# A fused attention and dense kernel: the probability product as one run of 56 matmuls, and priority shifts by step

## Chip, core and metric

The kernel runs on one core of a Trainium2 chip. The metric is the device time of one execution in microseconds (us); below, PE is TensorE, PEld its weight load, DVE VectorE, ACT ScalarE, POOL GpSimd and SP the SyncE queue that issues the DMAs.

## What is computed

```python
scores = scale * np.matmul(q, k.transpose(0, 1, 3, 2))     # 4 batches, 8 heads, 576 x 64
thresh = np.max(scores, axis=-1, keepdims=True) - tau
scores = np.where(scores >= thresh, scores, -1000000000.0)
attn = np.exp(scores - np.max(scores, axis=-1, keepdims=True))
attn = attn / (np.sum(attn, axis=-1, keepdims=True) + 1e-09)
x = np.matmul(attn, v)            # then heads side by side: 2304 tokens x 512
...
h = (x @ w1) * (x @ w2) @ w3      # 512 -> 1024 -> 1024
x = h @ w_out                     # 1024 -> 512
h = x @ w_in                      # 512 -> 2048
out = (h * (1.0 / (1.0 + np.exp(-h)))) @ w_out2
```

## The kernel before

**Stages.** The work is four batches of attention and then four groups of tokens through the dense layers. `merge` puts them in five stages: attention of batch 0 beside the product of w3 and w_out (line 1477); attention of batches 1, 2 and 3, each beside the dense layers of the group before; and the last group alone. In the profile the stages meet near 147, 378, 548 and 728 us.

**Attention.** Heads go in 16 pairs, four to a batch. A tile of 128 score rows is four or eight matmuls (line 867) into one of two PSUM buffers; DVE takes the maximum (line 834), ACT and DVE do mask and exponential (lines 900 to 926), then ACT and DVE write the probabilities as a high and a low half in 16 bits (lines 967 and 974), and SP's queue transposes them into the tiles `pt` (lines 985 and 994). When all tiles of a pair are there, `pv` (line 1009) multiplies them by the values: 14 chunks (9 of the high values, 5 of the low) x 2 halves of the tokens x 2 heads, 56 matmuls of 128 x 64 against 288 columns in 16 bits (line 1039). The two heads write the two halves of the partitions of one bank. ACT and DVE copy the result out as the next layer's input (lines 1063, 1078 and 1085).

**Dense layers.** They run in fp32r with each operand split in a high and a low part, three matmuls of 128 x 128 against 288 or 432 columns for each product (line 1426, and line 1376 in the last stage). Weights are split by ACT and POOL or DVE (lines 541, 565 and 559).

**Who sets the order.** Every operation is given to a planner with an engine, a duration and a priority. `Plan.run` simulates all engines: at each step it takes, of all operations whose inputs and buffers are there, the one that can start earliest, and among equal starts the one with the lowest priority number, which is the operation's place on a time scale of the stage (`plan.base`, in us of TensorE work). It leaves no engine idle while something is ready for it. The order so found is the fixed order of each engine's instructions on the chip. Only the order is taken over; the chip keeps its own time.

`pv` gives its 56 matmuls to the planner as five operations, of 3, 3, 3, 3 and 2 chunks, all with the same inputs and the same two banks. An operation that follows another one on PE is ready 3 ns after it:

```python
LATENCY = {
    ("PE", "PE"): 3, ("PE", "ACT"): 127, ("PE", "DVE"): 103,
```

The duration that the plan gives such an operation comes from

```python
def mm(n, width, f32r=False):
    return n * (width * 0.4517 + 2.9 if f32r else width * 0.4167 + 2.5) + 3
```

that is 1.03 x 738 = 760 ns for one of three chunks and 508 ns for the one of two, 3.55 us in all.

`merge` lays the steps of the attention and those of the dense layers over the same stretch of the time scale. Then it moves each step by a number of `SHIFTS`: eight numbers for the attention steps of a stage and eight for the dense ones, each for an eighth of the steps. A step is for example "the scores of two tiles", "the product of one pair" or "one output block of a dense layer"; the shift moves the priority of all its operations, on all engines and on SP's queue.

Of the kernel before, what the change touches and what calls it, by code (L numbers as in the profile page):

```python
# [17 lines left out]
HALF = S // 2  # L18
# [54 lines left out]
    (  # L73
        (3, -4, -5, -5, -15, -15, -6, 7),
        (-4, -3, 15, 9, 9, 0, -11, -4),
    ),
)

# [280 lines left out]
def fused_kernel(  # L359
# [11 lines left out]
    nc = tc.nc  # L371
    plan = Plan()
# [151 lines left out]
    def mm(n, width, f32r=False):  # L524
        return n * (width * 0.4517 + 2.9 if f32r else width * 0.4167 + 2.5) + 3
# [10 lines left out]
    def act_op(kind, n, fn, r, w, hold=(), ns=110):  # L536
        plan.op(kind, "ACT", ns + n * 0.833, fn, r, w, hold)
# [37 lines left out]
    def part_of(view):  # L575
        b = Buf()
        b.tile = view
        return b
# [5 lines left out]
    vst = [part_of(vs_all[:, j]) for j in range(2)]  # L584
    k_vx = [Buf(), Buf()]
# [423 lines left out]
    def pv(pr):  # L1009

        b, k = pr // NP, pr % NP
        got = [pts.pop(2 * pr + j) for j in range(2)]
        vs = vps[pr][1]
        ps = [m_b(1), m_b(1)]
        more = [p for p, _ in got]
        for g2, *_ in PLACES[b]:  # L1020
            if (g2, k) not in xs:
                new = x2_b if g2 == 2 else x_b
                xs[g2, k] = new(), new()
                more.extend(xs[g2, k])
        if b == 1:
            xs[2, k] = x2_b(), x2_b()
        if b == 2:
            wide[k] = x32_b()
        if b > 1:
            more.append(wide[k])  # L1030
        cs = [*((c, c) for c in range(9)), *((9 + c, c) for c in range(5))]
        for n0 in range(0, len(cs), 3):
            part = cs[n0:n0 + 3]

            def prods(part=part):
                for n, c in part:
                    for a in range(2):
                        for j in range(2):
                            nc.tensor.matmul(  # L1039
                                out=ps[a].t[64 * j:64 * j + 64, 0:HALF], lhsT=vst[j].t[:, n, :],  # L1040
                                rhs=got[j][0].t[:, c, a * HALF:(a + 1) * HALF],
                                start=(n == 0), stop=(n == len(cs) - 1),
                            )

            plan.op(
                "pv", "PE", 1.03 * mm(2 * len(part), HALF), prods,
                [*got[0][1], *got[1][1], *vst, *k_vx], ps, hold=more if n0 == 0 else more[:2],
            )

        def scales():  # L1050
            for i in range(2):
                m = slice(64 * i, 64 * i + 64)
                nc.vector.tensor_copy(out=vs.t[m, 8:9], in_=vs.t[m, 6 + i:7 + i])

        plan.op("v scale", "DVE", 140, scales, [vs], [vs])
        for a in range(2):
            if b == 3 or b == 2 and a == 1:
                at = HALF * (a + 1) if b == 3 else 0
                key = Buf()
                wkeys.setdefault(k, []).append(key)  # L1060
                act_op(
                    "x up", HALF,
                    lambda a=a, at=at: nc.scalar.activation(
                        out=wide[k].t[:, at:at + HALF], in_=ps[a].t[:, 0:HALF], func=ACTF.Copy,
                        scale=vs.t[:, 8:9],
                    ),
                    [ps[a], vs], [key], [wide[k]], ns=163,
                )
                continue
            (g2, c0, _, at), = PLACES[b]  # L1070
            at += a * HALF - c0
            xh, xl = xs[g2, k]
            kh, kl = Buf(), Buf()
            cut = slice(at, at + HALF)
            xkeys.setdefault((g2, k), []).append((at, at + HALF, kh, kl))
            act_op(
                "xh", HALF,
                lambda a=a, cut=cut, xh=xh: nc.scalar.activation(
                    out=xh.t[:, cut], in_=ps[a].t[:, 0:HALF], func=ACTF.Copy, scale=vs.t[:, 8:9],
                ),  # L1080
                [ps[a], vs], [kh], [xh], ns=163,
            )
            plan.op(
                "xl", "DVE", 436,
                lambda a=a, cut=cut, xh=xh, xl=xl: nc.vector.scalar_tensor_tensor(
                    out=xl.t[:, cut], in0=ps[a].t[:, 0:HALF], scalar=vs.t[:, 8:9],
                    in1=xh.t[:, cut].bitcast(F32), op0=ALU.mult, op1=ALU.subtract,
                ),
                [ps[a], kh, vs], [kl], [xh, xl],
            )  # L1090
        if b == 3 and k % 2:
            quads = [
                (
                    Buf(lambda _, w=w, i=i: wide[w].t[:, i * WIDE:(i + 1) * WIDE]),
                    wkeys[w][i:i + 2], wide[w],
                )
                for w in (k - 1, k) for i in range(2)
            ]
            xcs.append(combine(quads))
# [25 lines left out]
    def combine(quads):  # L1125

        (b11, n11, h1), (b12, n12, _), (b21, n21, h2_), (b22, n22, _) = quads
        hold = [*dict.fromkeys(x for x in (h1, h2_) if x is not None)]  # L1130
        psum = b11.tag == "m"

        def sub(out, a, b, need):
            plan.op(
                "c sub in PSUM" if psum else "c sub", "DVE", 75 + WIDE * 1.042,
                lambda: nc.vector.tensor_tensor(
                    out=tile_of(out), in0=tile_of(a), in1=tile_of(b), op=ALU.subtract
                ),
                [a, b, *need], [out], hold,
            )  # L1140

        if psum:
            s11, t1, t2 = u_b(), u_b(), u_b()
            plan.op(
                "y out", "ACT", 75 + WIDE * 0.833,
                lambda: nc.scalar.activation(out=s11.t, in_=tile_of(b11), func=ACTF.Copy),
                [b11], [s11],
            )
        else:
            s11, t1, t2 = b11, b12, b22  # L1150
        got = {"B11": parts(b11, n11, hold)}
        sub(t1, b12, s11, [*n12, *n11])
        got["B22"] = parts(b22, n22, hold)
        sub(t2, b22, t1, n22)
        got["T2"] = parts(t2, [], hold)
        sub(b11, t2, b11, n11)
        got["T3"] = parts(b11, [], hold)
        got["T1"] = parts(t1, [], hold)
        got["B21"] = parts(b21, n21, hold)
        sub(b21, b21, t2, n21)  # L1160
        got["T4"] = parts(b21, [], hold)
        return got

    def move_x(k):

        key = xkeys[1, k][1][2:]
        new = Buf(), Buf()
        c0, c1 = MOVED
        for a, b, k0, k1 in zip(xs[1, k], xs[2, k], key, new):
            act_op(  # L1170
                "x move", c1 - c0,
                lambda a=a, b=b: nc.scalar.activation(
                    out=b.t[:, 0:c1 - c0], in_=a.t[:, c0:c1].bitcast(F32), func=ACTF.Copy
                ),
                [k0], [k1], [a, b],
            )
        xkeys.setdefault((2, k), []).append((0, c1 - c0, *new))
# [622 lines left out]
    def merge(a, m, lead):  # L1800

        plan.stage += 1
        shifts = SHIFTS[plan.stage]
        ta, tm = sum(c for c, _ in a) or 1.0, sum(c for c, _ in m) or 1.0
        base = plan.base
        jobs = []
        for t, steps, off, late in ((ta, a, lead, shifts[0]), (tm, m, 0.0, shifts[1])):
            at = 0.0
            for n, (c, fn) in enumerate(steps):
                jobs.append((at / t * (ta + tm) - off, len(jobs), fn, late[8 * n // len(steps)]))  # L1810
                at += c
        for at, _, fn, late in sorted(jobs, key=lambda x: x[:2]):
            plan.base = base + at + late
            fn()
        plan.base = base + ta + tm
# [7 lines left out]
    for b in range(len(GROUPS)):  # L1823
# [9 lines left out]
        if pairs:  # L1833
# [5 lines left out]
            for grp in range(4):  # L1839
                for i in range(2):  # L1840
                    c = slice(grp % 2 * 512, grp % 2 * 512 + 512)
                    n = 16 + grp // 2 * 4 + 2 * i
# [11 lines left out]
    plan.base = 0.0  # L1854
    w34s = [(0.0, load_wo)] + [(6.9, lambda f=f: w34_step(f)) for f in range(8)]
    merge(attn_steps(0), w34s, LEAD)
    for i in range(len(GROUPS)):
        steps = [(0.0, lambda k=k: move_x(k)) for k in range(NP)] if i == 1 else []
        merge(attn_steps(i + 1) if i + 1 < B else [], steps + moe_steps(i), LEADS[i])
# [55 lines left out]
```

## Time and profile before

| | |
|---|---|
| Median of 3 runs | 979.19 us (979.11 to 982.52) |
| Profiled execution | 981.1 us |
| Its span, first to last instruction | 979.3 us |
| PE busy | 934.6 us |
| DVE busy | 693.0 us |
| ACT busy | 675.4 us |
| POOL busy | 447.9 us |
| TensorE's granted clock, mean over the span | 0.98 of full |

Busy time is the time in which an engine had an instruction running; matmuls are pipelined, so that time lost between them can lie inside PE's busy time. The profiled execution's own time holds the span and what lies around it.

### The profile page before, as it was taken

What the parts mean: (1) busy time and instruction counts of PE and PEld (TensorE: products, weight loads), DVE (VectorE), ACT (ScalarE), POOL (GpSimd) and SP (SyncE); (2) the same over time, 40 slices, a digit from 0 to 9 for tenths busy, and PEclk for the clock granted to TensorE, in tenths of its full rate; (3) what the DMA queues carried; (4) which work ended last, traced back from release to release, by engine and by line L of the source; (5) the groups of instructions that cost most, each with busy time, mean ns of one, the idle gap of its engine ahead of it and who ended that gap; (6) DMA issues with size and microseconds to landing.
All of it is one profiled execution on the core that took longest, in us unless ns stands there. A gap on an engine that the chain in (4) does not pass through costs nothing.

```text
span 979.3 us, 16087 instructions
## 1 busy us (share of the span) xinstructions
PE 934.6 (95%) x5632; PEld 830.2 (85%) x5632; DVE 693.0 (71%) x1488; ACT 675.4 (69%) x1217; POOL 447.9 (46%) x271
## 2 busy tenths in 40 slices
PE   4589999999999999999999999999999999999998
PEld 3455559989999989888889989899889999899998
DVE  6889676878887987666657766676459845856654
ACT  7989787878987877776878678887734423654331
POOL 1433233423341525575758567694776422423310
PEclk9589999999999999999999999999999999999999
DMA  8998999979899997787776878675632122111111
GB/s 247 244 257 231 254 298 306 268 215 279 256 257 259 241 251 217 174 208 182 171 173 181 235 170 207 176 182 139 140 123 85 44 67 85 44 65 65 51 36 73
DMA packets 216241, 175.13 MB, mean 179 GB/s; under 512 B 175584, under 2 KB 181728, under 8 KB 216160
## 3 DMA queue, kind: packets, MB, share of 16 engines
q1 hardware_dynamic: 216160, 174.10, 66.8%
q8 instruction: 44, 0.72, 0.3%
q14 instruction: 37, 0.30, 0.1%
HBM read 112.20 MB, written 19.40 MB: 134 GB/s over the span
## 4 chain that ended last, share of the span: by engine, by line
PE 75%; DVE 7%; DMA 6%; ACT 6%; issue 3%; POOL 1%; SPq 0%; ACTq 0%; DVEq 0%; POOLq 0%
PE banks L1426 45%; PE banks L1376 13%; PE banks L867 7%; PE banks L1039 7%; PE banks L1477 4%; DMA vr<-qkv 2%; DVE banks L834 2%; DMA pt<-hl 1%; DMA qk<-qkv 1%; DVE hm L974 1%; POOL lo L565 1%; DVE wr L1249 1%; DMA r<-w 1%; ACT banks L900 1%; ACT wr L1234 0%
## 5 line engine op out<-in xcount | busy, mean ns | idle before, releaser
L1426 PE MATMUL banks<-acts,hi 128*128 128x288 f32 (+1 forms) x1280 | 310.3, 330 | 0.8 <-ACT banks L900 0.8
L565 POOL TENSOR_TENSOR lo<-wr,hi 128x1024 fp32r<-128x1024 f32 x77 | 185.6, 2412 | 190.8 <-PE banks L1426 92.9
L1426 PEld LDWEIGHTS banks<-acts,hi 128*128 128x128 f32 x1280 | 219.0, 188 | 13.3 <-issue 7.0
L1426 PE MATMUL banks<-acts,lo 128*128 128x288 f32 (+1 forms) x640 | 209.3, 327 | 1.4 <-POOL lo L565 1.4
L867 PE MATMUL banks<-k,qs 128*128 128x288 f32 x640 | 122.8, 328 | 26.3 <-DVE e L926 8.8
L867 PEld LDWEIGHTS banks<-k,qs 128*128 128x128 f32 x640 | 100.0, 202 | 46.4 <-DVE e L926 8.7
L834 DVE TENSOR_REDUCE banks<-banks 128x1 f32<-128x576 f32 x144 | 107.0, 761 | 44.9 <-PE banks L867 43.3
L541 ACT ACTIVATE hi<-wr 128x1024 fp32r<-128x1024 f32 x96 | 101.9, 1062 | 33.9 <-DMA wr<-w 9.7
L1426 PEld LDWEIGHTS banks<-acts,lo 128*128 128x128 f32 x640 | 120.2, 188 | 5.3 <-POOL lo L565 2.4
L1426 PE MATMUL banks<-x,hi 128*128 128x288 f32 (+1 forms) x512 | 123.3, 329 | 0.0
L1426 PE MATMUL banks<-act3s,hi 128*128 128x432 f32 x384 | 106.8, 359 | 1.5 <-ACT act3s L1601 1.3
L565 POOL TENSOR_TENSOR acts<-tb,acts 128x432 fp32r<-128x432 f32 (+1 forms) x60 | 73.0, 1223 | 42.8 <-ACT acts L1515 35.2
L1426 PEld LDWEIGHTS banks<-x,hi 128*128 128x128 f32 x512 | 87.3, 188 | 3.8 <-issue 2.0
L565 POOL TENSOR_TENSOR qs<-qk,qs 64x576 fp32r<-64x576 f32 x31 | 45.4, 1463 | 95.7 <-ACT qs L661 77.0
L1426 PE MATMUL banks<-x,lo 128*128 128x288 f32 (+1 forms) x256 | 83.7, 327 | 1.4 <-POOL lo L565 1.1
L1426 PEld LDWEIGHTS banks<-act3s,hi 128*128 128x128 f32 x384 | 72.2, 188 | 5.4 <-ACT act3s L1601 1.6
L1039 PE MATMUL banks<-pt,vst 128*64 128x288 f16 x896 | 72.7, 297 | 4.3 <-DMA pt<-hl 3.6
L1039 PEld LDWEIGHTS <-vst 128*64 128x64 f16 x896 | 46.3, 112 | 30.0 <-issue 26.6
L1426 PE MATMUL banks<-act3s,lo 128*128 128x432 f32 x192 | 68.9, 359 | 0.0
L565 POOL TENSOR_TENSOR lo<-sums,hi 128x1024 fp32r<-128x1024 f32 x16 | 38.8, 2426 | 63.2 <-PE banks L1376 33.8
L1477 PE MATMUL banks<-wos,hi 128*128 128x512 f32 x128 | 62.8, 622 | 2.0 <-DVE hi L1249 2.0
L974 DVE SCALAR_TENSOR_TENSOR hl<-banks,st,hl 128x576 f16<-128x576 f32 x67 | 52.5, 811 | 16.2 <-ACT hl L967 16.0
(155 smaller groups left out, 1799.1 us busy)
## 6 DMA issues: line engine op xcount, KB each, us to landing
wr<-w SPq DMA_DIRECT2D x72, 512.0 KB, 3.8
qk<-qkv SPq DMA_DIRECT2D x31, 576.0 KB, 5.0
r<-wo SPq DMA_DIRECT2D x24, 512.0 KB, 6.2
w<-wr SPq DMA_DIRECT2D x24, 512.0 KB, 4.5
vr<-qkv SPq DMA_DIRECT2D x16, 576.0 KB, 5.3
r<-w3t SPq DMA_DIRECT2D x16, 512.0 KB, 6.1
r<-w SPq DMA_DIRECT2D x16, 512.0 KB, 7.5
r<-win SPq DMA_DIRECT2D x16, 512.0 KB, 6.8
```

What stands on the lines that cost most here:

```text
L541: kind, n, lambda: nc.scalar.activation(out=out(), in_=a(), func=ACTF.Copy), r, w, hold, ns
L565: lambda: nc.gpsimd.tensor_tensor(out=out(), in0=a(), in1=b(), op=ALU.subtract),
L834: lambda: nc.vector.tensor_reduce(out=low(), in_=sp.t[:, :, 0:HALF], axis=AX.XY, op=ALU.max, negate=True),
L867: nc.tensor.matmul(out=sp.t[:, a, 0:HALF], lhsT=q.t[:, o:o + 128], rhs=k.t[:, a * HALF:(a + 1) * HALF], start=(n == 0), stop=(n == len(mms ...
L900: lambda n=n, sp=sp, x=x: nc.scalar.activation(out=half2(x), in_=half2(sp), func=ACTF.Prelu, bias=col(1, n), scale=1.0, alpha=1.0e36,),
L974: lambda: nc.vector.scalar_tensor_tensor(out=two(hl.t[:, S:2 * S]), in0=src(), scalar=r(), in1=two(hl.t[:, 0:S]), op0=ALU.mult, op1=ALU.su ...
L1039: nc.tensor.matmul(out=ps[a].t[64 * j:64 * j + 64, 0:HALF], lhsT=vst[j].t[:, n, :], rhs=got[j][0].t[:, c, a * HALF:(a + 1) * HALF], start= ...
L1249: lambda: nc.vector.scalar_tensor_tensor(out=ri(), in0=low(), scalar=29, in1=ri(), op0=ALU.logical_shift_right, op1=ALU.bitwise_or,),
L1376: nc.tensor.matmul(out=ps.t[:, 0:n], lhsT=cut(w_), rhs=x_.t, start=(first and k == 0 and i == 0), stop=(k == len(quads) - 1 and i == 2), s ...
L1426: nc.tensor.matmul(out=ps.t[:, 0:n1 - n0], lhsT=a_.t[:, k * 128:(k + 1) * 128], rhs=x_.t[:, n0:n1], start=(n == 0 and i == 0), stop=(n == ...
L1477: lambda jb=jb, x=x: nc.tensor.matmul(out=ps.t[:, 0:512], lhsT=f32(r.t)[:, jb * 128:(jb + 1) * 128], rhs=x.t[:, 0:512].bitcast(F32), start ...
```

## The change

In `pv` the five operations become one, which issues all 56 matmuls one after the other. Its duration in the plan is the sum of its matmuls and 210 ns, 3.64 us. The operation holds all buffers that the five held between them.

In `merge` every step gets a further shift of its own, added to that of its eighth. These are the table `FINE`, some 310 numbers in the same unit, mostly between -30 and 30; its first and last lines are below. The operations, their engines and their number are else the same; the order of each engine's instructions is planned anew with both edits.

```diff
+FINE = (
+    (
+        (-22.5, 16, 2, 4, 5, 13, 5.5, 3.5, 1, 2, -1.5, -0.5, 1, 1.5, 1, 11.5,
...
+        (-10, 1, 5.5, 20.5, 10.5, 2.5, 0, 3.5, -12,),
+    ),
...
+    (
+        (),
+        (13, 8, 13, 28.5, 28.5, 22.5, 18.5, 19, 30, 34, 30.5, 37, 25.5, 11.5, -1, 32,
+         -57, 8, 24, -14.5, -18, -23, -66, -10, 5.5, 20, 58, 0, 8.5, 7,),
     ),
 )
...
         cs = [*((c, c) for c in range(9)), *((9 + c, c) for c in range(5))]
-        for n0 in range(0, len(cs), 3):
-            part = cs[n0:n0 + 3]
-
-            def prods(part=part):
-                for n, c in part:
-                    for a in range(2):
-                        for j in range(2):
-                            nc.tensor.matmul(
-                                out=ps[a].t[64 * j:64 * j + 64, 0:HALF], lhsT=vst[j].t[:, n, :],
-                                rhs=got[j][0].t[:, c, a * HALF:(a + 1) * HALF],
-                                start=(n == 0), stop=(n == len(cs) - 1),
-                            )
-
-            plan.op(
-                "pv", "PE", 1.03 * mm(2 * len(part), HALF), prods,
-                [*got[0][1], *got[1][1], *vst, *k_vx], ps, hold=more if n0 == 0 else more[:2],
-            )
+
+        def prods():
+            for n, c in cs:
+                for a in range(2):
+                    for j in range(2):
+                        nc.tensor.matmul(
+                            out=ps[a].t[64 * j:64 * j + 64, 0:HALF], lhsT=vst[j].t[:, n, :],
+                            rhs=got[j][0].t[:, c, a * HALF:(a + 1) * HALF],
+                            start=(n == 0), stop=(n == len(cs) - 1),
+                        )
+
+        plan.op(
+            "pv", "PE", mm(2 * len(cs), HALF) + 210, prods,
+            [*got[0][1], *got[1][1], *vst, *k_vx], ps, hold=more,
+        )
...
-        for t, steps, off, late in ((ta, a, lead, shifts[0]), (tm, m, 0.0, shifts[1])):
+        fine = FINE[plan.stage]
+        for t, steps, off, late, more in (
+            (ta, a, lead, shifts[0], fine[0]), (tm, m, 0.0, shifts[1], fine[1])
+        ):
             at = 0.0
             for n, (c, fn) in enumerate(steps):
-                jobs.append((at / t * (ta + tm) - off, len(jobs), fn, late[8 * n // len(steps)]))
+                jobs.append((
+                    at / t * (ta + tm) - off, len(jobs), fn, late[8 * n // len(steps)] + more[n]
+                ))
                 at += c
```

## Rows read from the trace of the kernel before

**Rows 1.** The page, part 1: busy us, share of the span and instructions of each engine.
```profile
PE 934.6 (95%) x5632; PEld 830.2 (85%) x5632; DVE 693.0 (71%) x1488; ACT 675.4 (69%) x1217; POOL 447.9 (46%) x271
```

**Rows 2.** The page, part 4: shares of the chain that ended last.
```profile
PE 75%; DVE 7%; DMA 6%; ACT 6%; issue 3%; POOL 1%; SPq 0%; ACTq 0%; DVEq 0%; POOLq 0%
```

**Rows 3.** Stretches by stage: busy us of each engine (instructions), granted clock, DMA.
```profile
core 0: us, PE busy (x) PEld busy (x) DVE busy (x) ACT busy (x) POOL busy (x), PEclk, DMA share, GB/s
0.00:75.00 75.00, 46.71 (x189) 31.99 (x190) 59.81 (x151) 64.90 (x119) 23.04 (x20) 0.77 0.93 250
75.00:147.40 72.40, 70.56 (x350) 38.19 (x348) 56.09 (x130) 62.58 (x116) 22.34 (x14) 0.98 0.99 262
147.40:378.00 230.60, 226.47 (x1758) 215.85 (x1757) 185.74 (x376) 186.36 (x346) 79.75 (x45) 1.00 0.95 258
378.00:548.00 170.00, 167.11 (x1024) 150.01 (x1024) 115.33 (x284) 129.83 (x226) 110.31 (x66) 1.00 0.75 185
548.00:728.00 180.00, 178.11 (x1071) 160.37 (x1070) 111.23 (x257) 133.00 (x235) 127.49 (x79) 1.00 0.68 170
728.00:979.30 251.30, 245.67 (x1249) 233.82 (x1247) 164.76 (x293) 98.77 (x180) 84.95 (x49) 1.00 0.19 63
```

**Rows 4.** TensorE's waits, whole span: line, releaser, us in total, times, longest.
```profile
PE banks L867 <- DVE e L926: 8.8, 5, 3.1
...
PE banks L867 <- DVE hm L974: 2.8, 3, 1.3
```

**Rows 5.** TensorE in order of time, one pair's probability product, third stage: start, us.
```profile
399.48 0.36 PE L1426 MATMUL banks<-x,lo 128*128 128x432 f32 x1
399.77 0.93 PE L1039 MATMUL banks<-pt,vst 128*64 128x288 f16 x12
400.62 0.66 PE L1426 MATMUL banks<-x,hi 128*128 128x432 f32 x2
...
403.91 0.78 PE L867 MATMUL banks<-k,qs 128*128 128x288 f32 x4
...
406.20 0.68 PE L1039 MATMUL banks<-pt,vst 128*64 128x288 f16 x8
406.81 0.66 PE L1426 MATMUL banks<-x,hi 128*128 128x432 f32 x2
```

**Rows 6.** The same view where two or three pieces stand together.
```profile
249.96 1.66 PE L1039 MATMUL banks<-pt,vst 128*64 128x288 f16 x24
251.55 0.53 PE L1426 MATMUL banks<-acts,hi 128*128 128x288 f32 x2
...
532.62 2.40 PE L1039 MATMUL banks<-pt,vst 128*64 128x288 f16 x36
534.94 0.79 PE L867 MATMUL banks<-k,qs 128*128 128x288 f32 x4
```

**Rows 7.** The same view, two matmuls of a product with no change of shape.
```profile
708.57 0.36 PE L1426 MATMUL banks<-acts,lo 128*128 128x432 f32 x1
708.77 0.56 PE L1426 MATMUL banks<-acts,hi 128*128 128x432 f32 x2
```

**Rows 8.** The same view, first and last of the 72 runs of line 1039.
```profile
39.97 0.45 PE L1039 MATMUL banks<-pt,vst 128*64 128x288 f16 x1
...
707.46 0.68 PE L1039 MATMUL banks<-pt,vst 128*64 128x288 f16 x8
```

**Rows 9.** TensorE in order of time, end of the first stage.
```profile
138.51 1.25 PE L1039 MATMUL banks<-pt,vst 128*64 128x288 f16 x12
141.56 0.90 PE L867 MATMUL banks<-k,qs 128*128 128x288 f32 x4 [1.80 <-DVE hl L974]
...
143.97 1.33 PE L867 MATMUL banks<-k,qs 128*128 128x288 f32 x4
145.23 2.27 PE L1039 MATMUL banks<-pt,vst 128*64 128x288 f16 x32
...
147.43 0.53 PE L1426 MATMUL banks<-x,hi 128*128 128x288 f32 x2
```

More of the change, by code (lines that the diff above doesn't have):

```diff
@@ L75 @@
         (-4, -3, 15, 9, 9, 0, -11, -4),
+    ),
+)
+FINE = (
+    (
[4 rows of a table added]
+    ),
+    (
[6 rows of a table added]
+    ),
+    (
[6 rows of a table added]
+    ),
+    (
[6 rows of a table added]
+    ),
+    (
+        (),
+        (13, 8, 13, 28.5, 28.5, 22.5, 18.5, 19, 30, 34, 30.5, 37, 25.5, 11.5, -1, 32,
+         -57, 8, 24, -14.5, -18, -23, -66, -10, 5.5, 20, 58, 0, 8.5, 7,),
     ),
@@ L1031, in pv @@
         cs = [*((c, c) for c in range(9)), *((9 + c, c) for c in range(5))]
-        for n0 in range(0, len(cs), 3):
-            part = cs[n0:n0 + 3]
-            def prods(part=part):
-                for n, c in part:
-                    for a in range(2):
-                        for j in range(2):
-                            nc.tensor.matmul(
-                                out=ps[a].t[64 * j:64 * j + 64, 0:HALF], lhsT=vst[j].t[:, n, :],
-                                rhs=got[j][0].t[:, c, a * HALF:(a + 1) * HALF],
-                                start=(n == 0), stop=(n == len(cs) - 1),
-                            )
-            plan.op(
-                "pv", "PE", 1.03 * mm(2 * len(part), HALF), prods,
-                [*got[0][1], *got[1][1], *vst, *k_vx], ps, hold=more if n0 == 0 else more[:2],
-            )
+        def prods():
[10 more added lines that the diff above has]
+            [*got[0][1], *got[1][1], *vst, *k_vx], ps, hold=more,
+        )
         def scales():
```

20 rows, old and new, of the table FINE are left out of this document.

## Prediction

> **What bounds the kernel now.** I read the page's busy shares first, then its chain, then the busy time by stage, then TensorE's waits, and last TensorE in order of time around line 1039. TensorE (PE) is busy 95% of the span and no other engine over 71% [rows 1]; three quarters of the chain that ended last is PE's own work [rows 2]. By stage [rows 3] the picture splits in two. In the first 75 us PE is busy 46.7 of 75: an opening in which the first scores wait for softmax steps and the clock is at half for a part. From 75 us on it idles 1.8, 4.1, 2.9, 1.9 and 5.6 us in the five stretches (width less busy time), the last of which holds the final store too; the clock is full from 147 us on. The waits that remain are short and of many kinds; the two largest with scores behind a DVE step of the softmax are 8.8 us in 5 times and 2.8 us in 3 [rows 4]. So after 75 us a microsecond taken out of PE's own work is a microsecond off the end, as long as the other engines can be 2% faster too. In the three stretches from 147 to 728 us ACT is busy 186.4 of 230.6, 129.8 of 170 and 133.0 of 180, at most 81%, and DVE likewise at most 81% [rows 3]; they can.
>
> What PE's busy share hides is in its order of time [rows 5]. One pair's 56 matmuls of line 1039 come as five pieces (12, 12, 12, 12, 8), and between them PE does three matmuls of a dense layer or four of a score tile. The plan's code says why: a piece may start 3 ns after the one before it, another ready operation at once, and the earlier start wins.
>
> **The price of a cut.** Leaving: a piece of 12 starts at 399.77 and the next other matmul at 400.62, 0.85 us; a piece of 8 takes 0.61 (406.20 to 406.81) [rows 5]. Pieces that happen to stand together take 1.59 for 24 and 2.32 for 36 [rows 6]. From 12 to 24 and on to 36 it grows by 0.735 each, so a pair of matmuls, which run side by side, takes 0.1225 us, and 0.855 - 6 x 0.1225 = 0.12 us is paid once per run, when PE leaves the shape. Entering: the last dense matmul before the piece starts 0.29 us ahead of it [rows 5], where within a dense product the same form is followed after 0.20 [rows 7]; 0.09 us more. A cut costs 0.21 us. I count 72 runs of line 1039 in the trace, the first at 39.97 and the last at 707.46 us [rows 8], 16 in the stage up to 147 us and 18, 18 and 20 in the next three; 16 would do, one for each pair.
>
> A rule of the Trainium skill bears on this. "TensorEngine Tiling (Array Packing)", Key Properties, says that changing the tiling mode drains the engine, and "TensorE: Matmul & The Clock Gate", Part 2, puts a drain at about 128 cycles. My estimate from these pages is two drains of 53 ns for a cut, 0.11 us, and 52 cuts would then be 5.6 us. The rows say about twice that, and the runs of 24 and 36, which paid the 0.12 once, decide for the rows.
>
> **Part 1, the uncut product.** In the three stages from 147 to 728 us, 18 + 18 + 20 - 12 = 44 cuts go, 44 x 0.21 = 9.2 us. These stages are PE-bound, so I take all of it. In the second and third pair of the first stage 8 more go, 1.7 us; PE idles only 1.8 of 72.4 us there, and I take it too. The four cuts of the first pair (by 53 us) and of the fourth lie among waits. For the first I take nothing: there PE waits for others anyway. For the fourth the price is another [rows 9]: after the first 12 matmuls PE stands 1.80 us, because score matmuls queued behind them wait for a DVE step, while 44 matmuls of the product stand behind those scores; then the clock has fallen, and four score matmuls take 0.90 and 1.33 us, where they take 0.78 elsewhere [rows 5]. From 138.51 to 147.43 are 8.9 us. One run of 56 takes 0.12 + 28 x 0.1225 = 3.55 us, two score tiles some 0.7 each, 5.0 together: at most 4 us come free. At the least nothing does, if the next product's inputs then come late. I take the middle, 2.
>
> The uncut run holds PE for 3.55 us. Scores that now slip in after 0.85 us can be up to 2.7 us later, and behind them the softmax chain of DVE and ACT. The cover is the dense products that PE has ready; without it, four pairs of a stage would cost 4 x 2.7 = 10.8 us. On the other side, the product ends sooner: in rows 5 the pair takes 7.0 us from first piece to end, uncut 3.55, so its results and the transposed probabilities' buffers come free some 3.5 us earlier.
>
> **Part 2, the shifts and the new cost of the product.** They add no instruction and take none away; they change which ready operation goes first on each engine, and SP's loads and transposes are reordered with them. No row shows their effect. Bounds: above, what PE idles from 147 us on, 14.5 us, less the final store; I take 6 as the most that a new order finds. Below, a score tile made late by 2.7 us once a pair for a few pairs: 5 us lost. The opening's 28.3 idle us could give some 4 or lose some 3 by what is converted first. Since such a new order also makes new waits in place of the old, and these numbers are fitted to a plan that prices the product nearer to the rows (3.64 us, where rows 5 give 3.55 and 0.09), I take a small gain of 1.
>
> **Sum.** 9.2 + 1.7 + 2 + 1 = 13.9 us. The profiled execution took 981.1 us (span 979.3 and 1.8 around it), 1.9 above the median of the runs, so it would become 967.2, and the median 979.2 - 13.9 = 965.3. I say 965.
>
> **Rivals.** (a) *The search finds more.* If the new order also takes the 6 from the later stages and 4 from the opening in place of 1, the time is 979.2 - 12.9 - 10 = 956. For it: the waits are many and short, and the opening is idle for more than a third. Against: the order before was tuned for the same waits.
>
> (b) *A cut is worth half.* The entry's 0.09 could come with the wait that heads every operation rather than with the change of shape, and the fourth pair's stall return elsewhere. Then 52 x 0.12 = 6.2 and 1 for the order: 972. The estimate from the pages gives 5.6 for the cuts, nearly the same. Against: the merged runs of rows 6.
>
> (c) *Given back in one stage.* One stage is bound by the softmax chain rather than by PE, and the longer run delays each of its pairs: 10.8 of the 13.9 come back, 976. The place would be the first stage from 75 us, where ACT is busy 62.6 of 72.4 (86%) and DVE 77%. The Trainium skill, "Perfetto Trace Analysis", Identifying the Most-Contended Engine, speaks for this too: it holds matmul busy time to be a poor measure of PE's headroom and the weight loads' busy share (with the share of peak) a better one. That share is 85% here [rows 1], which would leave PE more slack than 95% does. The stretches agree only in part: weight loads are busy 216 of 230.6 us in the second stage, 94% [rows 3].
>
> (d) *Slower.* Scores queue behind whole products and two of the four stages with attention in them become chain-bound: PE runs out of ready dense products before the last pair's results are there, and stands at the stage's end, as it did for 1.80 us at 139.7. Price 2 x 10.8 = 21.6 against the gain of 13.9: 987. It turns to slower by over 0.5% once the new waits pass 13.9 + 4.9 = 18.8 us. Against: from 147 to 728 us PE idled under 9 us in all, so there is always a product ready.
>
> That the change doesn't do what it says can hardly be: the 56 matmuls are issued by one operation, and PE takes its queue in order.
>
> **Numbers.** The forecast has 0.64 (its own range 960 to 971), (a) 0.11, (b) 0.06, (c) 0.12, (d) 0.07. About 0.5%, 4.9 us, is what a measurement of this kernel can tell from no change: faster is below 974.3, slower above 984.1. Forecast, (a) and (b) give faster, 0.81 less a little for the forecast's upper tail; (c) gives same; (d) slower. Range 955 to 976: it takes in (a), (b) and most of (c).
>
> **What would show it.** Line 1039 in 16 runs, each 56 matmuls from start to next start 3.55 us at full clock; its busy total falling from the sum of 72 runs by about 52 x 0.12 = 6 us; PE's busy time down by some 10 us, its idle after 147 us not above 14.5 us. If PE's busy falls so and the span does not, (c) or (d) holds, and the wait that grew should be scores behind DVE or ACT. If the stretch from 138 to 147 us keeps its stall under another name, the 2 us were wrong. If PE's idle before 75 us moves by more than 3 us either way, the shifts did more than I gave them.

## The result and the profile after

The kernel after takes 970.63 us (median of 4 runs, 966.86 to 973.09) against 980.03 for the kernel before beside it: ratio 0.9897, 95% interval 0.9857 to 0.9937, 9.4 us or 1.0% faster. A second set of runs (e4 below) gave 970.29 and the same ratio, 0.9873 to 0.9922. The profiled execution is the fastest of its set: 966.9 us, span 965.1. The one of before is 1.1 us over its median, so the two profiles below differ by 14.2 us where the medians differ by 9.4.

The page's busy time and clock per slice, after, to set beside [rows 1]:

```profile
PE 913.6 (95%) x5632; PEld 835.5 (87%) x5632; DVE 685.6 (71%) x1488; ACT 677.5 (70%) x1217; POOL 447.8 (46%) x271
...
PEclk9999989999999999999999999999999999999999
```

PE is busy 21.0 us less than before and idle 51.5 us instead of 44.7. The chain of work that ended last reads as before [rows 2]:

```profile
PE 75%; ACT 7%; DVE 6%; DMA 6%; issue 2%; POOL 2%; SPq 1%; ACTq 0%; POOLq 0%; DVEq 0%
```

The stretches by stage, cut at the first, 1344th, 2016th and 2688th dense matmul (columns as in [rows 3], whose cuts at 378 and 548 us lie 1 and 7 us beside those matmuls):

```profile
0.00:75.00 75.00, 43.21 (x184) 29.66 (x184) 54.89 (x146) 62.37 (x116) 23.36 (x20) 1.00 0.91 244
75.00:150.90 75.90, 68.18 (x354) 39.95 (x355) 56.58 (x134) 66.52 (x122) 24.33 (x16) 0.96 1.05 260
150.90:374.70 223.80, 220.80 (x1752) 216.32 (x1751) 184.97 (x377) 185.51 (x343) 78.16 (x44) 1.00 0.98 261
374.70:547.50 172.80, 169.68 (x1071) 160.08 (x1070) 119.12 (x304) 134.86 (x234) 113.89 (x67) 1.00 0.79 198
547.50:715.20 167.70, 167.18 (x1039) 157.03 (x1038) 102.72 (x239) 129.03 (x227) 123.58 (x76) 1.00 0.70 173
715.20:965.10 249.90, 244.53 (x1241) 232.44 (x1239) 167.31 (x293) 99.18 (x179) 84.53 (x50) 1.00 0.19 62
```

Counted by these matmuls (of line 1426, now 1462, in PE's order of time), the kernel's stages are

| stage | before | after | after, second profile (e4) |
|---|---|---|---|
| to the first dense matmul | 147.4 | 150.9 | 152.2 |
| to the 1344th | 229.5 | 223.8 | 223.2 |
| to the 2016th | 178.4 | 172.7 | 173.4 |
| to the 2688th | 172.4 | 167.8 | 168.8 |
| to the end | 251.5 | 249.9 | 250.0 |

The three stages with dense products and attention got 16.1 us shorter (14.9 in the second profile), the last 1.6; the first got 3.5 us longer (4.8). The waits of PE, against [rows 4]:

```profile
PE banks L905 <- DVE e L964: 14.8, 6, 4.3
PE banks L905 <- ACT e L938: 10.7, 8, 3.7
...
PE banks L1513 <- DVE hi L1285: 3.1, 1, 3.1
...
PE banks L905 <- DVE hm L1012: 1.2, 3, 0.7
```

The waits for DVE behind the softmax (e), 8.8 us before, are now 14.8, in both kernels all in the first stage; those for the score buffers (hm), which before were all in the second stage, fell from 2.8 to 1.2. The end of the first stage, the place of [rows 9], in order of time:

```profile
125.17 1.03 PE L905 MATMUL banks<-k,qs 128*128 128x288 f32 x4 [2.37 <-DVE e L964]
129.32 6.20 PE L1513 MATMUL banks<-wos,hi 128*128 128x512 f32 x10 [3.12 <-DVE hi L1285]
...
137.62 3.62 PE L1075 MATMUL banks<-pt,vst 128*64 128x288 f16 x56
...
150.91 0.42 PE L1462 MATMUL banks<-x,hi 128*128 128x288 f32 x2
```

The fourth pair's product is one run of 56 from 137.62, and the stall of 1.80 us before its scores is gone. But PE stood 2.37 and 3.12 us just ahead of it, for the softmax and for a converted weight, and 20 of the matmuls of w3 and w_out now come behind the run, so that the first dense matmul is at 150.91 instead of 147.43. Line 1039 is line 1075 now. It has 16 runs, and its group and two others read

```profile
L905 PE MATMUL banks<-k,qs 128*128 128x288 f32 x640 | 117.3, 321 | 33.0 <-DVE e L964 14.8
...
L1513 PE MATMUL banks<-wos,hi 128*128 128x512 f32 x128 | 59.6, 610 | 3.1 <-DVE hi L1285 3.1
L1075 PE MATMUL banks<-pt,vst 128*64 128x288 f16 x896 | 60.3, 290 | 1.1 <-DMA pt<-hl 0.8
```

The product's group fell from 72.7 to 60.3 us. The scores' group fell from 122.8 to 117.3 and that of w3 and w_out from 62.8 to 59.6 with the same work; in the second profile they are 118.7 and 61.6. One thing that differs for them is the granted clock in the first 75 us, 1.00 in both profiles after and 0.77 in the one before; it isn't the change that sets it (last section).

### The profile page after: what moved, and what is told of

Its sections match the earlier page's. It is cut to its first block, busy times and chain, and to the rows that moved or that the text cites. A ratio compares the mean times of both kernels' runs of the same rounds, so it can differ in the third digit from the quotient of the medians.

```text
span 965.1 us, 16094 instructions
## 1 busy us (share of the span) xinstructions
PE 913.6 (95%) x5632; PEld 835.5 (87%) x5632; DVE 685.6 (71%) x1488; ACT 677.5 (70%) x1217; POOL 447.8 (46%) x271
## 4 chain that ended last, share of the span: by engine, by line
PE 75%; ACT 7%; DVE 6%; DMA 6%; issue 2%; POOL 2%; SPq 1%; ACTq 0%; POOLq 0%; DVEq 0%
PE banks L1462 49%; PE banks L1412 11%; PE banks L905 7%; PE banks L1075 5%; PE banks L1513 3%; DMA wr<-w 2%; DMA r<-w3t 2%; DVE sums L1341 1%; POOL lo L603 1%; DVE banks L872 1%; DMA pt<-hl 1%; DMA r<-wo 1%; ACT banks L946 1%; ACT banks L938 1%; DMA vr<-qkv 1%
## 5 line engine op out<-in xcount | busy, mean ns | idle before, releaser
L905 PE MATMUL banks<-k,qs 128*128 128x288 f32 x640 | 117.3, 321 | 33.0 <-DVE e L964 14.8
L1462 PE MATMUL banks<-x,hi 128*128 128x288 f32 (+1 forms) x512 | 122.8, 328 | 1.2 <-DVE tb L1584 1.2
L1513 PE MATMUL banks<-wos,hi 128*128 128x512 f32 x128 | 59.6, 610 | 3.1 <-DVE hi L1285 3.1
L1075 PE MATMUL banks<-pt,vst 128*64 128x288 f16 x896 | 60.3, 290 | 1.1 <-DMA pt<-hl 0.8
L1075 PEld LDWEIGHTS <-vst 128*64 128x64 f16 x896 | 51.5, 111 | 10.1 <-issue 6.6
```

The costliest lines, as they stand in the source:

```text
L905: nc.tensor.matmul(out=sp.t[:, a, 0:HALF], lhsT=q.t[:, o:o + 128], rhs=k.t[:, a * HALF:(a + 1) * HALF], start=(n == 0), stop=(n == len(mms ...
L1075: nc.tensor.matmul(out=ps[a].t[64 * j:64 * j + 64, 0:HALF], lhsT=vst[j].t[:, n, :], rhs=got[j][0].t[:, c, a * HALF:(a + 1) * HALF], start= ...
L1462: nc.tensor.matmul(out=ps.t[:, 0:n1 - n0], lhsT=a_.t[:, k * 128:(k + 1) * 128], rhs=x_.t[:, n0:n1], start=(n == 0 and i == 0), stop=(n == ...
L1513: lambda jb=jb, x=x: nc.tensor.matmul(out=ps.t[:, 0:512], lhsT=f32(r.t)[:, jb * 128:(jb + 1) * 128], rhs=x.t[:, 0:512].bitcast(F32), start ...
```

## Experiments

**One half at a time (e1, e2).** e1 keeps the uncut product with its cost in the plan and sets the further shifts to zero:

```diff
-                    at / t * (ta + tm) - off, len(jobs), fn, late[8 * n // len(steps)] + more[n]
+                    at / t * (ta + tm) - off, len(jobs), fn, late[8 * n // len(steps)]
```

> The product as one run with its new cost in the plan, all further shifts at zero. If the cuts pay (0.21 us each): the stretches with dense products and attention (first dense matmul to the 1344th, to the 2016th, to the 2688th) each come out some 3 us shorter than before (229.7, 178.5 and 172.2 us there), and the time is 968 to 972. If most of the gain is the shifts' (the profile after is shorter by 5.8, 5.7, 4.6 and 1.7 in the stages from the second on, twice what the cuts explain): 975 or more. If the uncut run is what lengthens the first stage by 3.5 us, the first dense matmul stays at 150 us or later here too.

993.8 us, ratio 1.0139 (1.0111 to 1.0167): the uncut product alone makes the kernel slower by 13.7 us. Line 1075 stands in 16 runs, and PE is busy 926.5 us, 8.1 less than before; its idle time is 66.7 us instead of 44.7. Three stretches (columns as above), the largest of PE's waits, and the longest one of scores in PE's order of time:

```profile
151.90:388.10 236.20, 223.77 (x1739) 217.68 (x1738) 184.90 (x364) 180.82 (x333) 84.61 (x45) 0.98 0.92 249
388.10:566.60 178.50, 172.20 (x1072) 160.75 (x1071) 122.05 (x310) 134.95 (x236) 113.77 (x67) 1.00 0.81 190
566.60:744.40 177.80, 170.34 (x1038) 158.92 (x1037) 113.22 (x241) 127.97 (x227) 128.08 (x79) 0.97 0.67 165
```

```profile
PE banks L1462 <- POOL lo L603: 11.2, 5, 5.9
```

```profile
139.62 3.62 PE L1075 MATMUL banks<-pt,vst 128*64 128x288 f16 x56
148.90 3.25 PE L905 MATMUL banks<-k,qs 128*128 128x288 f32 x12 [5.66 <-DVE hm L1012]
```

PE idles 12.4, 6.3 and 7.5 us in the three stages where before it idled 4.1, 2.9 and 1.9 (by the cuts of [rows 3]), and 5.66 us in one piece at the end of the first stage, where score matmuls wait for the score buffer that a DVE step still reads. Dense matmuls wait 11.2 us for the low halves of weights from POOL (2.5 before), 5.9 of them at once in the fourth stage.

e2 has the five pieces of before, at their old cost, with the table of further shifts:

```diff
-        plan.op(
-            "pv", "PE", mm(2 * len(cs), HALF) + 210, prods,
...
+        for n0 in range(0, len(cs), 3):
+            part = cs[n0:n0 + 3]
...
+            plan.op(
+                "pv", "PE", 1.03 * mm(2 * len(part), HALF), prods,
```

> The further shifts with the product in five pieces as before, at the old cost. If the cuts pay and the shifts give 1 us: 977 to 981. If the shifts pay by themselves what the profile after leaves over (8.6 us from the second stage on, less what the first stage loses): 971 to 976. If the numbers fit only the order that goes with the uncut product, the shifts here do no good or harm: 980 or more.

1017.55 us, ratio 1.0382 (1.0355 to 1.0409). The shifts alone lose 37 us. Neither half helps; together they give 9.4. The table helps in the plan that the uncut product makes and harms in that of the pieces.

**The first stage's shifts, and the spread (e3, e4).**

```diff
-        fine = FINE[plan.stage]
+        fine = FINE[plan.stage] if plan.stage else ([0] * len(a), [0] * len(m))
```

> The kernel after with the further shifts of the first stage (attention of batch 0 and the product of w3 and w_out) at zero, all others kept. If these shifts lengthen the first stage: first dense matmul at 143 to 146 us instead of 150.9, and the time 963 to 967. If the uncut run does it, or the stage is as long by the softmax chain: 150 us or later and no change, 969 to 973.

991.45 us, ratio 1.0107 (1.0084 to 1.0130), 21 us slower than after. Both theories miss: the first dense matmul is at 152.3 us, so those shifts are not what lengthens the first stage; and the second and fourth stage, whose own shifts were kept, take 9.1 and 12.6 us longer than after (232.9 and 180.4). What a shift does in a later stage hangs on where the plan stands when it gets there. Nor is it the uncut run that makes the first stage long: with the same run the first dense matmul is at 151.9 us in e1, but at 146.4 in e8 and 144.0 in e9 (both below).

> The kernel after, unchanged, once more beside these. If the 966.9 to 973.1 of its runs is a spread of the kernel itself, the runs here spread as widely and the profile shows where (I expect the stretch up to the first dense matmul, where the clock falls, to differ from 150.9 us by 2 us or more). If it was that chip, they stand within 2 us.

967.6 to 972.0 us in 6 runs. The spread is the kernel's own; the two profiles differ by 1.3 us up to the first dense matmul and by 1.2 after it, less than I expected of the opening.

**The cut's price (e6, e7).** Both leave the order of after as it is; in the two traces every other instruction stands in the same order on its engine. Four small matmuls are put into each pair's product, in e6 after chunks 3, 6, 9 and 12 as here, in e7 four times behind the loop:

```diff
+                if n in (2, 5, 8, 11):
+                    nc.tensor.matmul(
+                        out=ps[0].t[:, 320:322], lhsT=ones.t, rhs=ones.t[:, 0:2], start=True, stop=True,
+                        skip_group_check=True,
+                    )
```

In e6 the small matmuls fall between the parts of a sum in the same bank, and its output isn't the product's.

> The kernel after with four extra matmuls of 128 x 128 against 2 columns in each pair's run, after chunks 3, 6, 9 and 12, into a free part of the same bank; the order of all else is unchanged. They cut the run into the five pieces of before. Against the next kernel, which has the same four matmuls behind the run: 64 cuts x 0.21 = 13.4 us longer if the price holds, 7 us if it is half, nothing if the price was that of the planner's interleaving. In the trace a pair should take 0.85 us longer from its first matmul to the end of the last extra one.

> The kernel after with the same four extra matmuls directly behind each pair's 56. They cost their own time, some 0.1 to 0.3 us each (the small matmul of line 702 is followed after 0.11 us), 64 of them: 6 to 20 us over the kernel after's 970, of which the difference to the kernel before this one is free.

e6 takes 991.68 us and e7 980.67: 11.0 us for 64 cuts, 0.17 each in the end time. In PE's order of time, e6:

```profile
411.34 0.38 PE L1081 MATMUL banks<-ones 128*128 128x2 f32 x2
411.66 0.93 PE L1075 MATMUL banks<-pt,vst 128*64 128x288 f16 x12
412.51 0.38 PE L1081 MATMUL banks<-ones 128*128 128x2 f32 x2
```

and e7:

```profile
405.95 1.05 PE L1081 MATMUL banks<-ones 128*128 128x2 f32 x8
406.87 0.78 PE L905 MATMUL banks<-k,qs 128*128 128x288 f32 x4
```

A small matmul in the run takes 0.32 us from its start to the piece behind it (411.34 to 411.66), behind the run a quarter of 0.92 (405.95 to 406.87), 0.23. The 0.09 between them is the entry, and the piece of 12 takes 0.85 again, with the 0.12 that is paid once a run in it: 0.21 us for a cut, as priced. Here no operation of the plan begins at a piece, so the entry's 0.09 isn't a wait at an operation's head. From its first matmul to the one behind the last small one a pair takes 5.29 us in e6 and 4.47 in e7 (medians of 16), 0.82 more where 0.85 was expected.

**The same order, uncut (e5, e9, e10).** Here the plan is that of before, and the pieces are merged as they are issued. In e5 and e9, the same kernel, the first piece issues all 56 matmuls; in e10 the last one does, with `n0 == 12`:

```diff
-            def prods(part=part):
-                for n, c in part:
+            def prods(n0=n0):
+                for n, c in cs if n0 == 0 else ():
```

In the traces of e9 and e10 every instruction but line 1039's own stands in the order of before on its engine.

> The kernel before with its own plan and order, in which the first of the five pieces issues all 56 matmuls and the other four issue nothing; no other instruction changes its place on its engine. If a cut costs 0.21 us and TensorE is the bound: 52 to 56 cuts less, PE busy about 10 us shorter, time 980.1 - 10.9 = 969 (967 to 972), with line 1039 in 16 runs. If the uncut run itself hurts the softmax chain (the 13.7 us that the uncut product with its new plan lost): 980 or more, with longer waits of PE for DVE and ACT. If a cut costs half: 974.

986.51 us, ratio 1.0051 (1.0029 to 1.0073). The rows below are those of e9.

> The kernel before in its own order with all 56 matmuls issued where the first piece stood; its first profile was taken in an execution with TensorE at less than half its pace throughout, so it is taken once more. Its other runs had a median of 986.5 against 982.3 of before. If the cuts were paid out and the scores that stood between the pieces, now behind the whole run, cost more than they gave: PE busy 8 to 11 us less than before, and its idle time 14 us or more longer, by waits of scores or of dense products for DVE, ACT or POOL. If a cut costs nothing: PE busy as before.

985.41 us, ratio 1.0046 (1.0026 to 1.0066). The page's busy time, three stretches and two waits of e9:

```profile
PE 923.3 (94%) x5632; PEld 839.2 (85%) x5632; DVE 695.3 (71%) x1488; ACT 673.3 (69%) x1217; POOL 446.4 (45%) x271
```

```profile
144.00:378.10 234.10, 223.81 (x1752) 217.49 (x1751) 188.30 (x383) 186.59 (x347) 80.84 (x46) 0.99 0.96 259
378.10:557.10 179.00, 173.24 (x1070) 161.48 (x1070) 122.20 (x304) 134.57 (x235) 113.59 (x67) 0.99 0.76 189
557.10:730.40 173.30, 167.08 (x1029) 154.58 (x1028) 107.23 (x237) 128.14 (x226) 123.51 (x77) 1.00 0.67 166
```

```profile
PE banks L867 <- DVE hl L974: 5.8, 5, 2.3
PE banks L867 <- DVE hm L974: 5.5, 6, 1.7
```

This is the experiment that tells most. PE is busy 11.3 us less: 4.0 in the first stage, where the granted clock of the first 75 us differs too (0.93, 0.77 before), and 7.4 in the three stages above. From start to start the cuts are paid out there in full: behind the first stage a piece of 12 takes 0.856 us to the next other matmul and a run of 56 takes 3.551, in the median, in every kernel here that has them, so that 44 cuts are 9.2 us. Yet the kernel is 4 to 5 us slower, since PE idles 58.7 us instead of 44.7.

The first stage isn't where it loses:

```profile
139.01 3.94 PE L1039 MATMUL banks<-pt,vst 128*64 128x288 f16 x56
142.88 1.32 PE L867 MATMUL banks<-k,qs 128*128 128x288 f32 x8
144.03 0.42 PE L1426 MATMUL banks<-x,hi 128*128 128x288 f32 x2
```

The fourth pair takes 5.0 us from its first matmul to the first dense one instead of 8.9 [rows 9], and the stage ends 3.4 us sooner. The three stages behind it are longer by 4.5, 0.6 and 1.0 us: their cuts give 9.2 us and their waits, with the slower clock behind some of them, take 15.3. PE's idle time there went from 4.1, 2.9 and 1.9 us to 10.3, 5.8 and 6.2, and the scores' waits for the buffer that a DVE step still reads (line 974, hl and hm) from 0.2 and 2.8 us to 5.8 and 5.5. One of them, at the place of [rows 5], in order of time, first e9 and then before:

```profile
400.51 3.62 PE L1039 MATMUL banks<-pt,vst 128*64 128x288 f16 x56
...
405.34 1.22 PE L867 MATMUL banks<-k,qs 128*128 128x288 f32 x8
...
415.31 2.82 PE L867 MATMUL banks<-k,qs 128*128 128x288 f32 x12 [2.28 <-DVE hl L974]
```

```profile
405.48 0.79 PE L867 MATMUL banks<-k,qs 128*128 128x288 f32 x4
...
413.38 1.75 PE L867 MATMUL banks<-k,qs 128*128 128x288 f32 x12
```

Before, the two score tiles between the pieces started at 403.91 [rows 5] and 405.48, and the next ones at 413.38 without a wait. In e9 both stand behind the run and start at 405.34, the first 1.4 us later. DVE's softmax steps behind them are 1.1 us later, and then one of DVE's steps (line 767, the low half of a later pair's values) meets one of POOL's; POOL and DVE, again first e9 and then before:

```profile
410.82 2.39 POOL L565 TENSOR_TENSOR lo<-wr,hi 128x1024 fp32r<-128x1024 f32 x1 [6.65 <-ACT hl L918]
410.99 2.56 DVE L767 SCALAR_TENSOR_TENSOR vst<-vr,vs,vst 128x320 f16<-128x320 f32 x1
414.44 1.54 DVE L974 SCALAR_TENSOR_TENSOR hl<-banks,st,hl 128x576 f16<-128x576 f32 x2
```

```profile
409.86 0.54 DVE L767 SCALAR_TENSOR_TENSOR vst<-vr,vs,vst 128x320 f16<-128x320 f32 x1
411.82 1.53 DVE L974 SCALAR_TENSOR_TENSOR hl<-banks,st,hl 128x576 f16<-128x576 f32 x2
```

Before, line 767 was over when POOL's step started at 411.33. In e9 it starts beside that step and takes 2.56 us instead of 0.54, line 974 is 2.6 us late, and the next scores, 12 in PE's queue, wait 2.28 us. 2.0 of the 2.6 us are the longer step; the rest is the lateness of the scores. Then the 12 scores take 2.61 us to the next matmul (at 417.92) where before they take 1.58 (to 414.96): the granted clock is 0.60 there, 1.00 before. Other waits need no such step: near 249 us the dense products that stood between the pieces start at 252.21 instead of 249.36, ACT and DVE wait for them, and the scores at 255.81 wait 1.74 us for line 974. Dense products that are ready stand behind the waiting scores, and PE takes its queue in order.

> The same with all 56 matmuls issued where the last piece stood: scores and dense products that stood between the pieces now go ahead of the run, nothing else changes its place. Nothing is queued later than before but the first four pieces themselves, and the run ends some 0.8 us sooner by the cuts. If the cuts pay wherever scores are not pushed back: 967 to 972. If any shift of TensorE's order against the other engines loses more than the cuts give: 980 or more, as with the run at the first piece.

989.66 us, ratio 1.0090 (1.0065 to 1.0115): worse, where I expected the gain. At the same pair:

```profile
410.21 2.05 PE L867 MATMUL banks<-k,qs 128*128 128x288 f32 x8 [2.73 <-DVE hm L974]
412.19 4.59 PE L1039 MATMUL banks<-pt,vst 128*64 128x288 f16 x56
```

Now the scores are ahead of the whole run and reach PE before their buffer is free: 2.73 us of standing, with the ready run behind them, which then takes 4.53 us (to 416.72) at a granted clock of 0.78. The four pieces before had been what PE did in that time. So the pieces' places suited the other engines' steps on both sides.

**What more work costs in that order (e12).** e9's kernel with the four small matmuls behind each run, as in e7.

> The kernel in before's order with the uncut run (985 to 986.5 us, PE idle 14 us longer than before) and four small extra matmuls behind each pair's run, 0.23 us each by the trace of the kernel after with the same four, 14.7 us of TensorE work in all. Behind the kernel after they cost 10.3 us. If in this order the scores wait for DVE and ACT anyway, so that TensorE's freed time only turns into waits: 0 to 5 us more than without them, 985 to 991. If TensorE's work is the bound here as in the kernel after: 10 us or more, 996 to 1001.

1001.77 us, ratio 1.0199 (1.0165 to 1.0234), 15 to 16 us over e5 and e9.

```profile
PE 936.1 (94%) x5760; PEld 853.0 (85%) x5760; DVE 694.7 (70%) x1488; ACT 672.8 (67%) x1217; POOL 446.0 (45%) x271
```

PE is busy 12.8 us more than in e9 and the time grows by more than that. My theory that freed time of PE only turns into waits there, so that added time would be free, falls. Scores and dense products that other engines wait for stand behind the run, so its length is on their path too: here a longer run was paid in full, while a shorter one was not given back.

**A price in the plan (e8, e11).** No instruction is added, taken away or changed; one number of the plan is. e8 is after with `mm(2 * len(cs), HALF) + 115` instead of `+ 210`, e11 is before with `1.05 * mm(...)` instead of `1.03`.

> The kernel after with one number of the plan changed: the uncut product is priced 95 ns lower (as long as the five pieces of before together). No instruction is added or taken away. If the shifts find good orders in general: within 3 us of the kernel after, 967 to 974. If the 310 numbers fit one single plan, so that any other price makes them random moves: 15 to 25 us lost, 985 to 995, like the kernel with only the first stage's shifts at zero (991).

> The kernel before with one number of its plan changed: a piece of the product is priced at 1.05 times its matmuls instead of 1.03, some 15 ns for a piece. No instruction is added or taken away and the pieces stay. If the order before was itself fitted to one single plan (the 80 shifts), any other price throws it over: 995 to 1010, some 20 us slower, as happened to the kernel after. If only the table of 310 numbers is so brittle: 977 to 984.

e8 takes 1001.42 us, ratio 1.0195 (1.0158 to 1.0232), 31 us more than after; e11 takes 1010.96, ratio 1.0306 (1.0283 to 1.0330). A change of 95 ns, and one of 15 ns a piece, in what the plan believes lose 30 us, a little more than I expected of either. That both kernels' shifts are fitted to one single plan each, so that a new plan from the old numbers is a random one, is how I read it; each kernel was tried with one other price only.

## Why the prediction held, and which steps of it did not

The forecast was 965, range 955 to 976; measured 970.6. The direction and the range held; the gain was 9.4 us where the sum had 13.9. One term of the sum, the 44 cuts, was right in size and cause. That the rest of it came out near is luck: the uncut product with its new plan loses 13.7 us (e1) where I had it gain 12.9, and the shifts give 23.5 (e1 against e4) where I had them give 1. These two errors nearly cancel.

*The price of a cut, 0.21 us:* right. The traces of e6 and e7 repeat it, and their end times give 0.17. The 0.12 isn't all paid on leaving, though: by the starts in the traces the first two matmuls of a run are followed after 0.147 us, the next pairs after 0.1225, and from the last two to the next other matmul it is 0.22. So some 0.025 of it are paid just behind the entry and 0.10 at the exit. The line's busy total fell by 12.4 us, not 6: the tail of each run's last matmul overlaps what follows and counts as well (0.93 us busy for 0.85 to the next start in [rows 5]), and 4.3 of the 12.4 lie in the first stage, where the clock differs. The Trainium skill's rule of a drain at a change of the tiling mode ("TensorEngine Tiling (Array Packing)", Key Properties) agrees with these traces as to where the time is lost; the estimate made from it, 0.11 us, is half of what they show. At each cut the number type changes with the shape, 32 bits to 16 and back, and no run here tells the two apart.

*44 cuts, 9.2 us in the three middle stages:* right, by the starts in every uncut kernel's trace (e9). The stages got 16.1 us shorter; the other 6.9 are the new order's.

*"A microsecond taken out of PE's own work is a microsecond off the end":* wrong for a kept order. e9 took the cuts out and came out 5 us slower. The step argued from PE's small idle time that a product is always ready. But that was so in an order in which each score tile had its place; "ready" work behind a waiting score tile in PE's queue covers nothing. The 2.7 us by which scores could come late was about right as a bound (1.4 at one pair shown, 2.85 for the dense products at the other), but it left out that late steps of DVE can meet steps of POOL and become longer, and that PE's clock can fall behind a wait.

*Part 2, a small gain of 1 from the shifts:* the step that failed most. I bounded them by PE's idle time in the order before (6 up, 5 down), as if that order were the starting point. It is not: the uncut product makes a new plan, whose order has 66.7 us of idle PE time (e1), and the shifts start from there. Measured from the order before, by the profiles, the new order gains 6.9 us in the middle stages and 1.6 in the last, more than the 6, and the first is 3.5 longer, where I gave the opening 3 at most; only the net is small. I had also counted the 8.8 us of waits for the softmax among those that remain from 75 us on; in the trace they all lie before.

*First stage, 1.7 and 2:* wrong for the kernel after, whose first stage is 3.5 to 4.8 us longer; the stall at the fourth pair went as said, and other waits came a little ahead of it. In the order before (e9) the stage got 3.4 us shorter, near the 3.7 of the sum, but all of it at the fourth pair (3.9, the most that I gave it); the eight cuts ahead of it gave nothing, for the pair starts at 139.01 instead of 138.51.

*Rivals:* (d) named the mechanism that decides, work behind a whole run: e5 and e9 end at 985 to 987, near its 987, and e1 beyond it. (c) put the loss into the first stage; in e9 that is the one stage that gains. What keeps the kernel after off (d) is the table of shifts, by e1, which differs from it in nothing else.

In the kernel after's own order the cuts can be put back: e6 against e7 loses 11.0 us for 64 of them, 9.6 for 56, about the whole 9.4. Between orders the uncut product is harder to price. Fitted: 980.0 with cuts, 970.6 without, but the latter has 310 more numbers to fit. Not fitted: 1010.96 and 1017.55 with cuts (e11, e2), 991.45, 993.8 and 1001.42 without (e3, e1, e8), 18.7 us apart in the mean. Both gaps have the sign of the 11 us of PE work; that they are its effect is argued, not shown, with so few orders. One rival stands untested: no run fits such a table to the plan of the five pieces, so how much a finer table alone would gain isn't known; e2 shows only that this table doesn't serve that plan. It also stays open which waits make a random order 20 to 30 us longer; the ones shown are scores for their buffers, in part behind steps of DVE that overlap POOL's, and others are for split weights and softmax steps. No version here beats the kernel after.

## What to carry to other kernels

Where PE changes between matmuls of 128 x 128 in 32 bits and of 128 x 64 in 16 bits, look at the start-to-start times at the change: busy time hides the price, and it comes back with every cut. In a kernel whose engines run fixed queues, taking work out of the bounding engine shifts every meeting with the others, and of the others among themselves; test the edit in the old order as well as in the new plan, and count on refitting the order before the gain is there. When a planner makes the order, first change one of its prices by a little and time that: here it moved the kernel by 30 us, three times the gain under study.

## What was not expected of the hardware

A step of DVE can take several times as long beside one of POOL. Of the 32 steps of line 767 in the trace of before, the 23 that overlap no step of POOL take at most 0.55 us; of the nine that do, four take 0.93 to 2.23. In e9 a shift of 1.1 us put the one at 410.99 us beside POOL, and it took 2.56.

The clock in the first 75 us had a mean of 0.77 in the profile before and 1.00 in the one after, and the first dense matmul still came 3.5 us later. The change didn't raise it: e9 has the order of before with 0.93, and e6 and e7, both with the order of after, have 0.82 and 1.00. In that stretch PE waits long for other engines: after, 10.3 us for ACT and 9.8 for DVE in the softmax of the scores alone.

A run of 128 x 64 costs at both ends, some 0.115 us on entering and 0.10 on leaving.
